# Projections of an attention and feed-forward kernel: x's tiles moved by 64 bytes, and 512 columns in one matmul instead of 256 in two

## The chip, the cores and the metric

The kernel runs on one core of a Trainium2 chip. The metric is the device time of one execution in microseconds (us), lower is better. Three runs of the kernel before took 1352.29, 1352.97 and 1356.74 us; the median is 1352.97 us.

## The reference, cut to what matters

```python
# attention inside chunks of 64 positions, 8 batches, 8 heads, 576 positions, head size 64
scores = scale * np.matmul(q_c, k_c.transpose(0, 1, 2, 4, 3))
attn = softmax(scores)                          # over the 64 keys of the chunk
x = np.matmul(attn, v_c) as (4608 tokens, 512)  # heads joined
# first feed-forward block: three projections of x, their maximum, one projection back
h = np.maximum(np.maximum(x @ w1, x @ w2), x @ w3)   # w1, w2, w3: 512 x 768
x = h @ w_out                                        # 768 x 512
# second block
h = np.maximum(x @ w_in, 0.0)                        # 512 x 2048
out = h * h @ w_out                                  # 2048 x 512
```

The change touches only the line with `x @ w1`, `x @ w2` and `x @ w3`.

## The kernel before, in words

The 4608 tokens are cut into 9 blocks of 512 (`NB`, `TB`). Each block's x is held transposed: the 512 model dimensions lie on the partitions in four pieces (`KD` = 4) and the 512 tokens lie along the free axis. To keep nearly full float32 precision, every operand of a matmul is split in two float32r parts, a rounded one ("h") and the rest ("l"), and a product is the sum of three: h by h, h by l, l by h.

The work has four stages, in this order on TensorE (PE): attention and the three projections of the first block (line 445, tile p), the way back (line 647, tile y), and the second block's two products (lines 543 and 594, tiles z and o). The last three are done by a seven-product scheme on halves, so their matmuls have 256 columns by nature.

A **projection** is one call of `proj` (line 450): for one block b, one of six groups f of 128 output features and one of the three weights w, it fills one PSUM tile of 128 x 512 out of four pieces k and three pairs of parts. Each pair is a **pass** here: one weight tile of 128 x 128 against the block's 512 tokens. `halves` (line 439) issues a pass as two matmuls of 256 columns (`HC` = 256), each with its own load of the same weights (LDWEIGHTS, engine row PEld). There are 9 x 6 x 3 = 162 projections of 12 passes; the first two, p000 and p001, are computed in two parts of 256 tokens (`parts=2`, line 775) so that they can start when half of the block is there.

x's two tiles per block, `xh` and `xl`, are made in `att_V` (lines 404 to 407) in the pool `ap`, two buffers each. `att_H` (line 426, ScalarE) and `att_L` (line 431, VectorE) fill them from PSUM, 128 tokens at a time. Other tiles share the buffers later on: `hr` (line 608), `h3` and `h4` (line 622), and the wide operands of lines 278 to 283. The weights lie in the pool `wp`, in tiles of 2048 bytes per partition.

Addresses within a partition matter below. In the program as built every tile of `wp` begins at a multiple of 128 bytes. The three small pairs of tiles at line 64 take 192 bytes, so every later tile of `ap`, x's among them, begins 64 bytes past a multiple of 128. All slices that the matmuls read begin a multiple of 128 bytes further in, with one exception: where `early` is 48, slices begin 48 words earlier (lines 281 to 283 and 623), which is at a multiple of 128 again. Those are few matmuls of lines 543, 594 and 647.

What sets the order: up to block 1 a list written by hand (`order`, line 784) under a manual schedule. From block 2 on the loop at line 856 issues one projection per slot, one step of attention in four of 18 slots, and as many steps as the table `PACE` says of the generators that split the later weights (`park`, `park_wo`); there the framework's scheduler orders each engine's instructions and queues. After each projection `p1_end` (line 470) takes the PSUM tile: ScalarE copies the first weight's result (line 474), VectorE takes the maximum with the second and third (lines 477, 481), and the result goes to DRAM by SyncE's queue (lines 487, 490, 502).

Of the kernel before, what the change touches and what calls it, by code (L numbers as in the profile page):

```python
# [11 lines left out]
F32R = mybir.dt.float32r  # L12
# [8 lines left out]
P = 128  # L21
D = 64
H = 8
TB = 512
HC = 256
# [4 lines left out]
KD = 4  # L30
# [2 lines left out]
NM = 14  # L33
NG = 4
EARLY = 48
NJ = NF1 // 2
BY_HEADS = (0, 1, 4,)
FO = [f for j in range(NJ) for f in (j, NJ + j)]
QN = (1, 2, 5, 6, 3, 7, 4)
# [5 lines left out]
def kernel(ctx: ExitStack, tc, qkv, w123, w_out, w_in2, w_out2, out):  # L45


    nc = tc.nc
# [3 lines left out]
    ap = ctx.enter_context(tc.tile_pool(name="ap", bufs=2))  # L52
# [3 lines left out]
    def ps_tile(tag, name):  # L56
        return ps.tile([P, 512], F32, tag=tag, name=name, bufs={"acc": 4, "p": 2, "at": 2}[tag])
# [161 lines left out]
    def park_wo():  # L219
# [4 lines left out]
        for f in range(NF1):  # L224
            h, j = divmod(f, NJ)
            parts = [main[2 * r + h][:, j, :] if j < 2 else rest[r][:, h, :] for r in range(2)]
# [47 lines left out]
    def operands(wide, name, early=0):  # L274

        if not wide:
            return {}
        ts = [[ap.tile([P, KD, TB], F32R, tag=t, name=f"{name}{t}{i}") for i in range(2)] for t in ("xh", "xl")]
        ops = {i: [halved(ts[j][i // 4][:, i % 4, :]) for j in range(2)] for i in range(1, 8)}
        if early:  # L280
            ops[1] = [
                halved(t[0].rearrange("p k n -> p (k n)")[:, TB - early:2 * TB - early]) for t in ts
            ]
        return ops
# [14 lines left out]
    x_t = {}  # L299
# [100 lines left out]
    def att_V(*ts, tag="at"):  # L400
        for t in ts:
            b = t // 4
            if b not in x_t:
                x_t[b] = (
                    ap.tile([P, KD, TB], F32R, tag="xh", name=f"xh{b}"),
                    ap.tile([P, KD, TB], F32R, tag="xl", name=f"xl{b}"),
                )
            xps_t[t] = ps_tile(tag, "X").rearrange("p (a q) -> p a q", a=4)
        ops = [(t, et_t.pop(t), v_t.pop(t)) for t in ts]
        for p in range(4):  # L410
            for c in range(2):
                for t, et, v in ops:
                    for j in range(2):
                        o = (j ^ t % 2) * D
                        q = (c ^ t % 2) * D
                        nc.tensor.matmul(  # L416
                            xps_t[t][j * D:j * D + D, p, c * D:c * D + D], lhsT=v[o:o + D, c, p, :],
                            rhs=et[o:o + D, p, q:q + D], start=True, stop=True,
                        )
        for t in ts:  # L420
            if t >= 8:
                att_H(t)

    def att_H(t):
        o = t % 4
        nc.scalar.copy(x_t[t // 4][0][:, :, o * P:o * P + P], xps_t[t])
# [7 lines left out]
    def mm_k(dst, wpair, xpair, k, first, last):  # L434

        (wh, wl), (xh, xl) = wpair, xpair
        halves(dst, ((wh, xh), (wh, xl), (wl, xh)), first, last)

    def halves(dst, pairs, first, last):


        for j, (lhs, rhs) in enumerate(pairs):
            for i in range(dst.shape[-1] // HC):
                c = slice(i * HC, i * HC + HC)
                nc.tensor.matmul(  # L445
                    dst[:, c], lhsT=lhs, rhs=rhs[:, c], start=first and i == 0 and j == 0,
                    stop=last and j == len(pairs) - 1, skip_group_check=True,
                )

    def proj(wpair, xpair, name, parts=1, tag="p"):  # L450

        p = ps_tile(tag, name)
        wh, wl = wpair
        xh, xl = xpair
        n = TB // parts
        for i in range(parts):
            t = slice(i * n, i * n + n)
            for k in range(KD):
                a, c = k // 2, slice(k % 2 * P, k % 2 * P + P)
                mm_k(p[:, t], (wh[:, a, c], wl[:, a, c]), (xh[:, k, t], xl[:, k, t]), k, k == 0, k == KD - 1)  # L460
            if i + 1 < parts:
                yield None
        yield p


    h_t, st = {}, {}
    h_d = [dp.tile([7, P, NJ, HC], F32, name=f"hd{b}") for b in range(NB)]
    y_d = [dp.tile([P, KD, TB], F32, name=f"yd{b}") for b in range(NB)]
# [56 lines left out]
    def split_y(b, parts):  # L525

        ops = y_t[b] = operands(b % 2 == 1, "y", EARLY if b == 1 else 0)
        q = [parts[k][:, :, n * HC:n * HC + HC] for k in range(2) for n in range(2)]
# [40 lines left out]
    def load_g(b, g):  # L569
        parts = []  # L570
        for row in range(2):
            t = ap.tile([P, 2, 512], F32, tag="in", name="gr", bufs=4)
            nc.sync.dma_start(t, g_d[b][g, row])
            parts.append(t)
        return parts

    def split_g(parts, wide, early):

        ops = operands(wide, "g", early)
        q = [halved(parts[k][:, m, :]) for m in range(2) for k in range(2)]  # L580
        yield ops
        for i, x in combine(q, True, nc.vector):
            split_into(ops, i, x, "g")
            yield
# [16 lines left out]
    def load_h(b, part):  # L601
# [5 lines left out]
        for k in pairs:  # L607
            t = ap.tile([P, KD, TB], F32R, tag="xh", name="hr").bitcast(F32).rearrange("p k n -> p (k n)")
            t = t[:, 0:6 * HC].rearrange("p (i j n) -> p i j n", i=2, j=NJ)
            nc.sync.dma_start(t, h_d[b][k:k + 2].rearrange("i p j n -> p i j n"))  # L610
            raw_h[b, k], raw_h[b, k + 1] = t[:, 0], t[:, 1]
        for k in one:
            t = ap.tile([P, 2, 512], F32, tag="in", name="hr", bufs=4).rearrange("p k n -> p (k n)")
            t = t[:, 0:3 * HC].rearrange("p (j n) -> p j n", j=NJ)
            nc.sync.dma_start(t, h_d[b][k])
            raw_h[b, k] = t

    def split_h(b):

        for k, i in enumerate(QN):  # L620
            if i in (3, 4):
                t = ap.tile([P, KD, TB], F32R, tag="xl", name=f"h{i}").rearrange("p k n -> p (k n)")
                o = TB - (EARLY if b % 3 == 0 and i == 3 else 0)
                ts = [t[:, o + m * TB:o + m * TB + TB] for m in range(3)]
# [12 lines left out]
    def yq(b, i, tag, first):  # L637
# [5 lines left out]
        for a in range(2):  # L643
            c = slice(a * P, a * P + P)
            for j in range(NJ):
                for k, (l, r) in enumerate(((wh, hh), (wh, hl), (wl, hh))):
# [44 lines left out]
    def steps(t0, t1):  # L691
# [19 lines left out]
        def outputs(t):  # L711
            att_V(t, t + 1)
            att_L(t)
            att_L(t + 1)
            if t < 12:
                att_load(t + 4)
                att_load(t + 5)
            if t + 2 < t1:
                scores(t + 2)
# [20 lines left out]
    first = tc.manual_schedule()  # L740
# [4 lines left out]
    def tile_steps(k):  # L745

        att_load(k)
        yield
        att_S(k, tag="acc")
        yield  # L750
        m, n = (by_heads if k in BY_HEADS else att_M)(k), att_N(k)
        for _ in range(2):
            next(m)
        yield
        next(m, None)
        yield
        for _ in range(2 if k in BY_HEADS else 3):
            next(n)
        yield
        next(n, None)  # L760
        yield
        tp = att_T(k, "at")
        yield
        att_E(k, tp)
        yield
        att_V(k, tag="acc")
        yield
        att_H(k)
        yield
        att_L(k)  # L770
        yield
# [29 lines left out]
    for token in order:  # L801
# [6 lines left out]
        kind, n = token.rstrip("0123456789"), token.lstrip(ascii_letters)  # L808
# [10 lines left out]
        else:  # L819
            b, f, w = map(int, n)  # L820
# [35 lines left out]
    for b in range(2, NB):  # L856
        for slot in range(3 * NF1):
            f, w = divmod(slot, 3)
# [23 lines left out]
    last = None  # L882
# [43 lines left out]
    for b in range(NB):  # L926
        for g in range(NG):
# [27 lines left out]
            if b == NB - 1 and g == 0:  # L955
                parts = {j: load_g(*groups[j]) for j in range(2)}
                more = split_g(parts.pop(0), True, EARLY)
                ops = next(more)
# [67 lines left out]
```

## Time and profile before

| what | value |
|---|---|
| time of three runs | 1352.29, 1352.97, 1356.74 us |
| median | 1352.97 us |
| span of the profiled execution (the page gives no other time of it) | 1354.5 us |
| PE busy | 1337.8 us, 99% of the span |
| VectorE (DVE) busy | 979.8 us, 72% |
| ScalarE (ACT) busy | 556.9 us, 41% |
| GpSimd (POOL) busy | 178.4 us, 13% |
| bytes moved by DMA | 282.92 MB, mean 209 GB/s |

How to read it: the span runs from the first to the last instruction of the profiled execution. A matmul's row has a start and a duration, but matmuls are pipelined, so durations overlap and a busy share near 100% says nothing about how fast columns go in. The rate is read from the distance between the starts of two matmuls that follow each other. PEld is the row of the weight loads, which run beside the matmuls.

### The profile page before, as it was taken

The page shows a single profiled execution, that of the slowest core. Times are in us where ns is not written, and L with a number is a line of the kernel's source. Part 1 is how long each engine was busy: PE and PEld are TensorE (multiplying, and loading weights), DVE is VectorE, ACT ScalarE, POOL GpSimd, SP SyncE. Part 2 cuts the span into 40 slices and gives each one's busy share as a digit, 9 for nine tenths or more (in the row PEclk, how much of TensorE's full clock was granted, in tenths as well). Part 3 has the DMA queues.
Part 4 walks back from the last instruction along what each step waited for, and adds up shares of the span by engine and source line. Part 5 has one row for each costly group of instructions (what it writes and reads, how often), then busy time and mean ns, then how long its engine had stood idle before and what let it go on. Part 6 is the DMA issues. An engine that isn't in the chain of part 4 may idle for free.

```text
span 1354.5 us, 33080 instructions
## 1 busy us (share of the span) xinstructions
PE 1337.8 (99%) x13536; PEld 1325.1 (98%) x13537; DVE 979.8 (72%) x1661; ACT 556.9 (41%) x1047; POOL 178.4 (13%) x165
## 2 busy tenths in 40 slices
PE   7999999999999999999999999999999999999998
PEld 6999999999999999999999999999999999999998
DVE  6777789778898843566666666666777887887774
ACT  5632344344444422565433333333344453454442
POOL 2321035342344300000000000000001000000000
PEclk8999999999999999999999999999999999999999
DMA  9445779899788778998944333433597444443440
GB/s 271 124 140 158 227 228 313 256 319 292 256 284 270 253 253 301 381 308 270 294 167 143 122 139 135 149 140 141 211 355 284 148 147 137 144 156 125 141 141 32
DMA packets 146631, 282.92 MB, mean 209 GB/s; under 512 B 14384, under 2 KB 57008, under 8 KB 146480
## 3 DMA queue, kind: packets, MB, share of 16 engines
q1 hardware_dynamic: 146208, 280.55, 61.1%
q8 instruction: 106, 1.74, 0.5%
q14 instruction: 45, 0.37, 0.1%
q10 hardware_dynamic: 272, 0.26, 0.1%
HBM read 164.50 MB, written 116.26 MB: 207 GB/s over the span
## 4 chain that ended last, share of the span: by engine, by line
PE 91%; DVE 4%; DMA 3%; issue 1%; ACT 1%; SPq 0%; POOLq 0%; DVEq 0%; ACTq 0%
PE p L445 29%; PE z L543 25%; PE o L594 25%; PE y L647 8%; PE X L416 1%; DMA k<-in_qkv 1%; PE S L334 1%; PE T L388 1%; DMA hr<-hd 1%; DMA yr<-yd 0%; DMA wo20d<-pl 0%; DVE sm L373 0%; DVE e L361 0%; DVE e L382 0%; DVE a L107 0%
## 5 line engine op out<-in xcount | busy, mean ns | idle before, releaser
L543 PE MATMUL z<-yh,wih 128*128 128x256 f32 x560 | 154.7, 276 | 0.0
L543 PE MATMUL z<-yl,wih 128*128 128x256 f32 x560 | 154.6, 276 | 0.0
L543 PE MATMUL z<-yh,wil 128*128 128x256 f32 x560 | 154.6, 276 | 0.0
L594 PE MATMUL o<-wo2h,gxl 128*128 128x256 f32 x504 | 139.1, 276 | 0.0
L594 PE MATMUL o<-wo2h,gxh 128*128 128x256 f32 x504 | 139.1, 276 | 0.0
L594 PE MATMUL o<-wo2l,gxh 128*128 128x256 f32 x504 | 139.1, 276 | 0.0
L594 PE MATMUL o<-wo2h,gh 128*128 128x256 f32 x504 | 139.1, 276 | 0.0
L594 PE MATMUL o<-wo2l,gh 128*128 128x256 f32 x504 | 139.1, 276 | 0.0
L594 PE MATMUL o<-wo2h,gl 128*128 128x256 f32 x504 | 139.1, 276 | 0.0
L566 DVE TENSOR_TENSOR c<-z,s 128x512 f32<-128x512 f32 x108 | 74.3, 688 | 77.7 <-PE z L543 74.0
L566 POOL TENSOR_TENSOR u<-u,s 128x512 f32<-128x512 f32 x9 | 12.5, 1389 | 845.2 <-DVE u L566 674.7
L543 PE MATMUL z<-yxh,wih 128*128 128x256 f32 x448 | 123.8, 276 | 0.0
L543 PE MATMUL z<-yxh,wil 128*128 128x256 f32 x448 | 123.7, 276 | 0.0
L543 PE MATMUL z<-yxl,wih 128*128 128x256 f32 x448 | 123.7, 276 | 0.0
L551 ACT COPY s<-z 128x512 f32<-128x512 f32 x108 | 63.5, 588 | 139.0 <-PE z L543 124.2
L543 PEld LDWEIGHTS z<-yh,wih 128*128 128x128 f32 x560 | 105.1, 188 | 0.2 <-DVE c L566 0.2
L543 PEld LDWEIGHTS z<-yh,wil 128*128 128x128 f32 x560 | 105.1, 188 | 0.0
L543 PEld LDWEIGHTS z<-yl,wih 128*128 128x128 f32 x560 | 105.1, 188 | 0.0
L119 POOL TENSOR_TENSOR q<-a,r 128x256 uint32<-128x256 uint32 x76 | 66.6, 898 | 223.4 <-DVE a L107 100.1
L594 PEld LDWEIGHTS o<-wo2h,gxl 128*128 128x128 f32 x504 | 94.6, 188 | 0.0
L594 PEld LDWEIGHTS o<-wo2h,gxh 128*128 128x128 f32 x504 | 94.6, 188 | 0.0
L594 PEld LDWEIGHTS o<-wo2l,gxh 128*128 128x128 f32 x504 | 94.6, 188 | 0.0
(175 smaller groups left out, 4113.0 us busy)
## 6 DMA issues: line engine op xcount, KB each, us to landing
gd<-g SPq DMA_DIRECT2D x144, 256.0 KB, 2.0
gr<-gd SPq DMA_DIRECT2D x72, 512.0 KB, 3.6
qk<-in_qkv SPq DMA_DIRECT2D x28, 512.0 KB, 4.9
hr<-hd SPq DMA_DIRECT2D x17, 768.0 KB, 6.5
raw<-in_w_out SPq DMA_DIRECT2D x22, 512.0 KB, 4.6
hr<-hd SPq DMA_DIRECT2D x29, 384.0 KB, 5.8
raw<-in_w SPq DMA_DIRECT2D x18, 512.0 KB, 5.0
v<-in_qkv SPq DMA_DIRECT2D x72, 128.0 KB, 4.0
```

The source lines that it names most:

```text
L119: nc.gpsimd.tensor_tensor(out=part.bitcast(U32), in0=au[:, c], in1=ru[:, c], op=ALU.add)
L334: nc.tensor.matmul(s_t[t][o:o + D, h ^ t % 2, :], lhsT=q[r, h, :], rhs=k[r, h, :], start=True, stop=True,)
L388: nc.tensor.transpose(tp[:, p * P:(p + 1) * P], e[:, 2 * p:2 * p + 2, :].rearrange("p h k -> p (h k)"), ident)
L416: nc.tensor.matmul(xps_t[t][j * D:j * D + D, p, c * D:c * D + D], lhsT=v[o:o + D, c, p, :], rhs=et[o:o + D, p, q:q + D], start=True, stop= ...
L445: nc.tensor.matmul(dst[:, c], lhsT=lhs, rhs=rhs[:, c], start=first and i == 0 and j == 0, stop=last and j == len(pairs) - 1, skip_group_ch ...
L543: nc.tensor.matmul(dst[:, a * HC:a * HC + HC], lhsT=l[:, a, w], rhs=r[:, k, :], start=first and a + k + j == 0, stop=j == 2, skip_group_ch ...
L551: nc.scalar.copy(t, bank[tag])
L566: (eng or nc.vector).tensor_tensor(out=t, in0=x, in1=y, op=ALU.add)
L594: nc.tensor.matmul(bank[i][:, m * HC:m * HC + HC], lhsT=l[:, a, t], rhs=r[:, a, :], start=g + m + a + j == 0, stop=g == NG - 1 and j == 2, ...
L647: nc.tensor.matmul(dst[:, a * HC:a * HC + HC], lhsT=l[j][:, c], rhs=r[j], start=first and a + j + k == 0, stop=k == 2, skip_group_check=True,)
```

## The change

A new constant `SHIFT` = 16 (words of 4 bytes). `xh` and `xl` are allocated 32 words longer and used from word 16 on, so that x begins at a multiple of 128 bytes, as the weights do. `halves` is gone: `mm_k` issues each pass as one matmul of the width of its target, 512 columns, or 256 in the two projections of two parts. The order of the three pairs and of the pieces k stays.

```diff
@@ -33,6 +33,7 @@
 EARLY = 48
+SHIFT = 16
 NJ = NF1 // 2
@@ -401,9 +402,9 @@
             if b not in x_t:
-                x_t[b] = (
-                    ap.tile([P, KD, TB], F32R, tag="xh", name=f"xh{b}"),
-                    ap.tile([P, KD, TB], F32R, tag="xl", name=f"xl{b}"),
+                x_t[b] = tuple(
+                    ap.tile([P, KD * TB + 2 * SHIFT], F32R, tag=t, name=f"{t}{b}")[:, SHIFT:SHIFT + KD * TB]
+                    .rearrange("p (k n) -> p k n", k=KD) for t in ("xh", "xl")
                 )
@@ -434,18 +435,12 @@
         (wh, wl), (xh, xl) = wpair, xpair
-        halves(dst, ((wh, xh), (wh, xl), (wl, xh)), first, last)
-
-    def halves(dst, pairs, first, last):
-
-
+        pairs = (wh, xh), (wh, xl), (wl, xh)
         for j, (lhs, rhs) in enumerate(pairs):
-            for i in range(dst.shape[-1] // HC):
-                c = slice(i * HC, i * HC + HC)
-                nc.tensor.matmul(
-                    dst[:, c], lhsT=lhs, rhs=rhs[:, c], start=first and i == 0 and j == 0,
-                    stop=last and j == len(pairs) - 1, skip_group_check=True,
-                )
+            nc.tensor.matmul(
+                dst, lhsT=lhs, rhs=rhs, start=first and j == 0, stop=last and j == len(pairs) - 1,
+                skip_group_check=True,
+            )
```

Of the 162 projections 160 change: 160 x 12 = 1920 passes, which are 3840 matmuls and 3840 weight loads before and 1920 of each now. The 48 matmuls of 256 columns of p000 and p001 stay, with x at its new place. Lines up to 435 move down by one; line 445 becomes 440, and lines behind it move up by five.

On PE the instructions keep their places. This is the end of one projection and the beginning of the next in the list written by hand (w_0h and w_0l are the two parts of a weight tile, T the transposes and X the products of the attention); before:

```order
L445 MATMUL p_714<-xh_325,w_0h 128x256 x2
L445 MATMUL p_714<-xl_326,w_0h 128x256 x2
L445 MATMUL p_714<-xh_325,w_0l 128x256 x2
L388 MATMUL T<-ident,e 128x128 x4
L416 MATMUL X<-et,v 64x64 x32
L445 MATMUL p_799<-xh_325,w_1h 128x256 x2
L445 MATMUL p_799<-xl_326,w_1h 128x256 x2
L445 MATMUL p_799<-xh_325,w_1l 128x256 x2
```

and now:

```order
L440 MATMUL p_714<-xh_325,w_0h 128x512
L440 MATMUL p_714<-xl_326,w_0h 128x512
L440 MATMUL p_714<-xh_325,w_0l 128x512
L389 MATMUL T<-ident,e 128x128 x4
L417 MATMUL X<-et,v 64x64 x32
L440 MATMUL p_787<-xh_325,w_1h 128x512
L440 MATMUL p_787<-xl_326,w_1h 128x512
L440 MATMUL p_787<-xh_325,w_1l 128x512
```

Each pair of rows has become one of double width; nothing has moved.

On DVE the scheduler puts some rows of blocks 2 to 7 in another order. The first place is in block 2, where the maximum h of a projection, the scaling of two attention tiles (e by rs) and the conversion of later weights (a) are interleaved; before:

```order
L382 TENSOR_TENSOR e<-e,rs 128x512
L378 RECIPROCAL rs<-sm 128x8
L104 TENSOR_SCALAR a<-a 128x512
L382 TENSOR_TENSOR e<-e,rs 128x512
L481 TENSOR_TENSOR h<-p_2525,m_2507 128x512
L107 SCALAR_TENSOR_TENSOR a<-raw,a 128x512
```

and now:

```order
L383 TENSOR_TENSOR e<-e,rs 128x512
L379 RECIPROCAL rs<-sm 128x8
L476 TENSOR_TENSOR h<-p_2057,m_2039 128x512
L383 TENSOR_TENSOR e<-e,rs 128x512
L105 TENSOR_SCALAR a<-a 128x512
L103 TENSOR_SCALAR a<-a 128x512
```

The maximum h has moved ahead of the second scaling of e, and one conversion behind it; no row is added or lost.

## Rows read from the trace of the kernel before

**Rows 1.** The page: span, busy times, and granted clock in 40 slices.
```profile
span 1354.5 us, 33080 instructions
PE 1337.8 (99%) x13536; PEld 1325.1 (98%) x13537; DVE 979.8 (72%) x1661; ACT 556.9 (41%) x1047; POOL 178.4 (13%) x165
...
PEclk8999999999999999999999999999999999999999
...
PE p L445 29%; PE z L543 25%; PE o L594 25%; PE y L647 8%; PE X L416 1%; DMA k<-in_qkv 1%; PE S L334 1%; PE T L388 1%; DMA hr<-hd 1%; DMA yr<-yd 0%; DMA wo20d<-pl 0%; DVE sm L373 0%; DVE e L361 0%; DVE e L382 0%; DVE a L107 0%
```
**Rows 2.** Line 445 alone: count, duration ns min/median/max, first and last start in us.
```profile
L445 PE MATMUL p<-xh,w_0h x216: 276/276/384, 29.6 to 491.1; 128*128 128x256 f32 x108
```
**Rows 3.** Waits of PE, 29 to 510 us: us in total, times, longest.
```profile
PE T L388 <- DVE e L382: 1.6, 2, 1.1
PE p L445 <- issue: 1.0, 2, 0.6
PE p L445 <- DVE m L477: 0.5, 1, 0.5
```
**Rows 4.** Chain of work that ended last: start us, us, what, number of instructions.
```profile
153.21 8.18 PE p L445 x72
```
**Rows 5.** Timeline of PE in block 1: start us, us, engine, line, what.
```profile
59.88 0.40 PE L445 MATMUL p<-xh,w_1h 128*128 128x256 f32 x2
...
61.77 0.40 PE L445 MATMUL p<-xh,w_1l 128*128 128x256 f32 x2
```
**Rows 6.** Windows, line 445 alone: stretch, its us, PE busy (matmuls), PEld, clock, DMA.
```profile
38.00:120.00 82.00, 77.37 (x648) 76.57 (x648) 1.00 0.48 146
120.00:160.00 40.00, 32.61 (x278) 31.89 (x279) 1.00 0.54 174
163.00:187.00 24.00, 22.64 (x188) 22.26 (x188) 1.00 0.61 185
```
**Rows 7.** Timeline of PE in block 2, across a wait of PE.
```profile
163.69 0.39 PE L445 MATMUL p<-xl,w_1h 128*128 128x256 f32 x2
163.92 0.39 PE L445 MATMUL p<-xh,w_1l 128*128 128x256 f32 x2
164.70 0.50 PE L445 MATMUL p<-xh,w_1h 128*128 128x256 f32 x2 [0.39 <-issue]
165.04 0.40 PE L445 MATMUL p<-xl,w_1h 128*128 128x256 f32 x2
```
**Rows 8.** Timeline of PE, line 543, operands 64 bytes apart modulo 128.
```profile
799.78 0.28 PE L543 MATMUL z<-yxh,wil 128*128 128x256 f32 x1
...
800.12 0.28 PE L543 MATMUL z<-yxh,wil 128*128 128x256 f32 x1
...
802.95 0.28 PE L543 MATMUL z<-yxh,wih 128*128 128x256 f32 x1
```
**Rows 9.** Timelines of PE, lines 543 and 594, operands at one offset modulo 128.
```profile
700.63 0.28 PE L543 MATMUL z<-yxh,wih 128*128 128x256 f32 x1
...
702.05 0.29 PE L543 MATMUL z<-yxh,wih 128*128 128x256 f32 x1
...
1008.63 0.28 PE L594 MATMUL o<-wo2h,gxh 128*128 128x256 f32 x1
...
1010.08 0.28 PE L594 MATMUL o<-wo2h,gxh 128*128 128x256 f32 x1
```
**Rows 10.** Timeline of PE, second and fourth warm-up matmul at full clock.
```profile
7.62 0.38 PE L732 MATMUL warm<-zero 128*128 128x512 bf16 x1
...
8.05 0.38 PE L732 MATMUL warm<-zero 128*128 128x512 bf16 x1
```
**Rows 11.** Timeline of PEld, line 543: weight loads beside the matmuls of rows 8.
```profile
800.12 0.19 PEld L543 LDWEIGHTS z<-yxh,wih 128*128 128x128 f32 x1
```
**Rows 12.** Windows, all engines: PE, PEld, DVE, ACT, POOL busy, clock, DMA share, GB/s.
```profile
188.00:220.00 32.00, 31.30 (x420) 30.71 (x413) 28.94 (x48) 13.36 (x26) 15.45 (x14) 1.00 0.86 291
...
252.00:284.00 32.00, 31.41 (x385) 31.01 (x384) 29.38 (x58) 14.10 (x25) 14.38 (x15) 1.00 0.82 265
```
**Rows 13.** Groups of instructions: count, busy us, mean ns, idle before.
```profile
L481 DVE TENSOR_TENSOR h<-p,m 128x512 f32<-128x512 f32 x54 | 36.8, 684 | 17.2 <-PE p L445 16.5
L382 DVE TENSOR_TENSOR e<-e,rs 128x512 f32<-128x512 f32 x28 | 19.2, 685 | 0.2
```
**Rows 14.** Groups on PE from 38 to 120 us: count, busy us, mean ns.
```profile
L445 PE MATMUL p<-xl,w_2h 128*128 128x256 f32 x48 | 9.6, 281 | 0.0
```

## The prediction

> **What bounds the kernel now.** I read the page first. PE is busy 1337.8 of 1354.5 us, and in the chain that ended last line 445, the projections, has 29% [rows 1]. The granted clock is at its upper level, 2.4 GHz, in all slices but the first, so 256 columns need at least 256 / 2.4 = 106.7 ns and 512 need 213.3 ns. Line 445 runs from 29.6 to about 508 us; one of its 18 operand names has 216 matmuls [rows 2], together 18 x 216 = 3888. PE waits for others in that stage for only about 4 us, 1.6 of them for VectorE [rows 3]. So the stage is bound by how fast PE takes projections, and what a pass saves or costs comes out nearly whole at the end: the later stages start when this one is through, and they are PE's too.
>
> How long does a pass take? Starts are what counts. Over 72 matmuls of the chain it is 8.18 / 72 = 113.6 ns each [rows 4], so a pass of two takes 227.2 ns. But there is a second pace: between 59.88 and 61.77 us there are 16 matmuls, 1.89 / 16 = 118.1 ns each [rows 5], a pass 236.2 ns. It lasts: the stretches 38 to 120 and 163 to 187 us run so, the one between them does not [rows 6], and the trace shows one change of pace right behind a wait of 0.39 us: steps of 0.23 us for two matmuls before it (163.69 to 163.92) and 0.24 after [rows 7]. The clock is 1.00 on both sides. I take it that the order in time of a weight load's reads and the running matmul's reads settles into one of two patterns.
>
> Addresses matter too. Line 543 with weights and moving data 64 bytes apart modulo 128 takes (802.95 - 799.78) / 28 = 113.2 ns [rows 8]. The few matmuls whose slices begin 48 words early, so that both operands lie at one offset, take (702.05 - 700.63) / 12 = 118.3 ns on line 543 and (1010.08 - 1008.63) / 12 = 120.8 ns on line 594 [rows 9]. Being at one offset costs 5 to 8 ns for 256 columns. This is the arrangement that the change gives the projections.
>
> The Trainium skill ("TensorE: Matmul & The Clock Gate", Part 2, step 1) says that TensorE reads weights and moving data through two independent ports and that loading the next weights takes nothing from the running matmul. By that rule the offset would be without effect and the shift worth 0; rows 9 against rows 8 disagree, by 5 to 8 ns, so the sum below doesn't use it, and its result stands as a rival.
>
> **The change part by part.** Now: the slow stretches hold 648 + 188 = 836 matmuls of line 445 [rows 6]; 24 of them are second parts of p000 and p001 and stay at 256 columns, the other 812 are 406 passes. 406 x 236.2 + 1514 x 227.2 ns = 95.9 + 344.0 = 439.9 us for the 1920 passes.
>
> One instruction for 512 columns: no float32r matmul of 512 columns stands in the trace, so its pace is bounded. Below: the warm-up matmuls have 512 columns, though of bf16: two steps from 7.62 to 8.05 us, 215 ns each [rows 10]; it can't be under 213.3. Above: nothing overlaps better than now and the same-offset price falls on every 256 columns, 2 x 120.8 = 241.6 ns. I take 213.3 ns for the columns and once what a 256-column matmul shows beyond its columns, 113.2 - 106.7 = 6.5 ns: 219.8 ns. This is nearest to the warm-up row, the only one of 512 columns. It supposes that the shift removes what the offset costs at this length, or that the price is hidden: the weight load now starts with the matmul, both at 800.12 us [rows 8, 11], and uncovered it takes 384 - 276 = 108 ns (the longest and the median duration of rows 2: the first matmul behind another shape has to wait for its weights). Beside 106.7 ns of columns it has no room to slip; beside 213.3 ns it has 105 ns. And the slow pace should go, since it needs a load that is only just in time. 1920 x 219.8 = 422.0 us, a gain of 17.9 us.
>
> 1920 weight loads and 1920 matmuls less to issue: nothing on PE waits for its sequencer beyond 1.0 us in this stage [rows 3], so I cost that at 0; it is covered by the running columns.
>
> The 48 matmuls of p000 and p001 stay short and come to one offset: 48 x 5 ns = 0.2 us more.
>
> VectorE's new order: where h goes ahead of the second scaling of e, that e is late by one row of 0.68 us [rows 13], and PE's transposes wait for e; today they do so twice, 1.6 us in all [rows 3]. In return h gives its PSUM tile back earlier, by the 0.69 us of e. The cover is the projections between. I take 1 us, with 0 and 2 as ends. SyncE's and GpSimd's queues change places of neighbours only; their transfers are waited for by later steps, and I take 0. ScalarE and VectorE write x 64 bytes further, the same number of elements: 0.
>
> Sum: 1354.5 - 17.9 + 0.2 + 1.0 = 1337.8 us of span. The profiled execution lies 1.5 us over the median of the runs, 1352.97; taken off, **1336.3 us**. Its own range, with 215 ns and with 222 ns a pass: 1327 to 1341.
>
> **The rivals.**
>
> *The load is hidden whole.* With 105 ns to spare, a collision only delays the load, and the columns run at the pace of rows 10: 1920 x 215 = 412.8 us, a gain of 27.1, 1327.1 us. For it: a load of 108 ns beside columns of 106.7 ns explains the 113 ns without any loss in the columns. Against it: in the slow stretch the matmuls' own rows last 281 ns instead of 276 [rows 14, 2], so the columns were held up as well. The skill's two ports (above) would give the same time. 0.18.
>
> *The price is per instruction, and the shift brings the dearer one.* If the running columns are held up once per weight load, as rows 9 may be read, a pass costs 213.3 + (120.8 - 106.7) = 227.4 ns: 436.6 us, a gain of 3.3, 1350.9 us: the two halves of the change cancel. For it: nothing in rows 9 shows that the same offset is ever good. Against it: rows 9 are of matmuls that have no room for the load. 0.18.
>
> *Slower: the price is per column.* If operands at one offset hold the columns up all along, 512 columns cost 2 x 118.3 to 2 x 120.8 = 236.6 to 241.6 ns: 454.3 to 463.9 us, 14.4 to 24.0 us more, so 1354.5 + 14.4 + 1.2 - 1.5 = 1368.6 to 1378.2 us. The place is every pass of line 440; it decides from 228.5 ns a pass on, (439.9 - 1.2) / 1920, where gain turns to loss. For it: rows 9 are the only ones with the operands so placed, and all are slower than their neighbours; float32r columns need twice the bytes of the bf16 columns of rows 10, so that row may promise too much. Against it: a weight load lasts 108 ns, and the second half of a long matmul has none beside it. 0.22.
>
> *VectorE becomes the bound.* It is busy 28.94 and 29.38 of 32 us in two stretches [rows 12], 0.90 and 0.92; a stage shorter by 17.9 / 440 = 4% brings that to 0.96. If each of the 12 pairs of attention tiles from block 3 on made PE wait 0.8 us, the mean of the two waits in rows 3, 9.6 us would go back: 1345.9 us. 0.05.
>
> **How the numbers follow.** The forecast has 0.37. The time predicted is that of the forecast, 1336 us. About 0.3%, 4 us, is what a measurement of this kernel can tell from no change. Faster by more: forecast, hidden load and VectorE, 0.37 + 0.18 + 0.05 = 0.60; within: 0.18; slower: 0.22. The range reaches down to the hidden load, 1327, and up into the slower rival, to 1372, which leaves out its dearer half, 0.11, and a few hundredths below.
>
> **What would show it.** Steps between starts on line 440: near 220 ns the forecast is right, 215 the hidden load, 227 the cancelling, 236 or more the slower rival. In the windows of 38 to 120 us there should be no second pace; if matmuls of one projection differ from those of another by 4% at clock 1.00, the patterns are still there. Lines 543, 594 and 647 should keep 113 ns. Waits of PE for VectorE above 3 us before the way back would speak for the last rival. The prediction is wrong if the passes take over 228.5 ns, or if PE's waits in this stage grow by more than 10 us.

## The result and the profile after

The changed kernel takes 1367.03 us (median of 6 runs, 1365.52 to 1369.32); the kernel before took 1354.62 us beside it (6 runs). The ratio is 1.0095, 95% interval 1.0079 to 1.0110: **the change makes the kernel slower by about 12 us**. The prediction was 1336.0 us, faster, with a range of 1327 to 1372.

The page of the changed kernel has these lines in the places of [rows 1]: span and busy times, granted clock, chain by line.

```profile
span 1363.5 us, 29241 instructions
PE 1349.3 (99%) x11616; PEld 1255.0 (92%) x11617; DVE 973.2 (71%) x1661; ACT 556.4 (41%) x1047; POOL 185.2 (14%) x165
...
PEclk9999999999999999999999999999999999999999
...
PE p L440 32%; PE z L538 26%; PE o L589 25%; PE y L642 8%; PE X L417 1%; PE S L335 1%; DMA k<-in_qkv 1%; PE T L389 1%; DMA yr<-yd 1%; SPq L308 0%; DVE e L362 0%; DVE mx L359 0%; DVE sm L374 0%; DVE e L383 0%; DVE xl L432 0%
```

The clock is at its upper level in all slices and PE is busy 99% as before, so the added time is time in which PE works more slowly. Which stage? The chain of the changed kernel (start us, us, what, number of instructions) has one long piece for each of the last two stages:

```profile
664.09 350.66 PE z L538 x2988
...
1017.61 337.58 PE o L589 x2977
```

and the chain of the kernel before has the same pieces:

```profile
666.80 338.96 PE z L543 x2988
...
1008.68 337.49 PE o L594 x2977
```

Here the loss stands: stage z, whose instructions the change doesn't touch, goes from 338.96 to 350.66 us, **11.7 us more**; stage o stays. Ahead of stage z the changed kernel is 2.7 us earlier (664.09 against 666.80), of which the projections have 1.1: they run from 27.8 to 529.5 us (501.7) where they ran from 29.6 to 532.4 us (502.8; the prediction's "about 508" for their end was misread). -2.7 + 11.7 = 9.0 us is the difference of the two spans, 1363.5 and 1354.5. The medians differ by 12.4 because the two profiled executions lie on different sides of them. A run's time is some 2 us more than its span: the profiled execution of the changed kernel took 1365.52 us, 1.5 under its median of 1367.03, and that of before about 1356, some 2 above 1354.62.

Stage z is slower matmul by matmul. The groups of instructions (count, busy us, mean ns) of the changed kernel:

```profile
L538 PE MATMUL z<-yh,wih 128*128 128x256 f32 x560 | 156.9, 280 | 0.0
...
L589 PE MATMUL o<-wo2h,gxh 128*128 128x256 f32 x504 | 139.2, 276 | 0.0
```

In the timeline of PE one sees where it begins:

```profile
696.34 0.28 PE L538 MATMUL z<-yl,wih 128*128 128x256 f32 x1
...
697.70 0.28 PE L538 MATMUL z<-yl,wih 128*128 128x256 f32 x1
...
697.93 0.28 PE L538 MATMUL z<-yxh,wih 128*128 128x256 f32 x1
...
701.47 0.28 PE L538 MATMUL z<-yh,wih 128*128 128x256 f32 x1
```

Up to 697.70 us there are 12 steps of 1.36 / 12 = 113.3 ns, from 697.93 on 30 steps of 3.54 / 30 = 118.0 ns. The first 12 of these are the first early slices, the 12 behind them the first that lie in a moved buffer. The stage stays at this pace. The windows of 740 to 780 us (stretch, its us, PE busy and matmuls, clock, DMA share, GB/s) of the changed kernel and of the kernel before:

```profile
740.00:780.00 40.00, 40.00 (x342) 1.00 0.34 124
```

```profile
740.00:780.00 40.00, 40.00 (x355) 1.00 0.37 136
```

342 matmuls instead of 355 in 40 us, at the same clock 1.00 and with less DMA traffic, not more. The waits of PE from 27 to 510 us (us in total, times, longest) answer to [rows 3] and have not grown:

```profile
PE T L389 <- DVE e L383: 1.8, 3, 1.1
PE p L440 <- DVE xl L432: 0.4, 1, 0.4
```

The passes of the projections, at last, run at two paces that change with the block. From the chain, 36 passes in blocks 2, 3 and 4:

```profile
150.36 8.17 PE p L440 x36
...
205.69 8.37 PE p L440 x36
...
262.07 8.17 PE p L440 x36
```

8.17 / 36 = 226.9 ns and 8.37 / 36 = 232.5 ns; over all of them the mean is 229.6 ns.

### The profile page after: what moved, and what is told of

It is laid out like the page before. It is cut to its first block, busy times and chain, and to the rows that moved or that the text cites. A ratio compares the mean times of both kernels' runs of the same rounds, so it can differ in the third digit from the quotient of the medians.

```text
span 1363.5 us, 29241 instructions
## 1 busy us (share of the span) xinstructions
PE 1349.3 (99%) x11616; PEld 1255.0 (92%) x11617; DVE 973.2 (71%) x1661; ACT 556.4 (41%) x1047; POOL 185.2 (14%) x165
## 4 chain that ended last, share of the span: by engine, by line
PE 94%; DMA 2%; DVE 2%; ACT 1%; issue 0%; SPq 0%; POOLq 0%; DVEq 0%; ACTq 0%
PE p L440 32%; PE z L538 26%; PE o L589 25%; PE y L642 8%; PE X L417 1%; PE S L335 1%; DMA k<-in_qkv 1%; PE T L389 1%; DMA yr<-yd 1%; SPq L308 0%; DVE e L362 0%; DVE mx L359 0%; DVE sm L374 0%; DVE e L383 0%; DVE xl L432 0%
## 5 line engine op out<-in xcount | busy, mean ns | idle before, releaser
L120 POOL TENSOR_TENSOR q<-a,r 128x256 uint32<-128x256 uint32 x76 | 73.6, 991 | 216.0 <-DVE a L108 104.4
L589 PEld LDWEIGHTS o<-wo2h,gh 128*128 128x128 f32 x504 | 94.6, 188 | 0.0
```

The source lines that it names most:

```text
L120: nc.gpsimd.tensor_tensor(out=part.bitcast(U32), in0=au[:, c], in1=ru[:, c], op=ALU.add)
L589: nc.tensor.matmul(bank[i][:, m * HC:m * HC + HC], lhsT=l[:, a, t], rhs=r[:, a, :], start=g + m + a + j == 0, stop=g == NG - 1 and j == 2, ...
```

## What differs between the blocks, and between the two stages z

Two buffers of x take turns block by block. The change makes each of the two tiles 32 words longer, so a tile's buffers lie 8320 bytes apart instead of 8192, and 8320 is 128 past a multiple of 256. Call the **distance** of a step the place where the running matmul's moving operand begins, less the place where the weights begin that are loaded beside it for the next matmul, modulo 256 bytes, from the addresses in the program as built. It counts modulo 256, not modulo 128 as was said ahead of the result. In the projections and in stages y and z the weights begin 128 bytes past a multiple of 256 in every kernel built here, so that there the distance changes with the moving operand's own place alone:

| steps | kernel before | changed kernel |
|---|---|---|
| projections (line 445, 440) | 192: all | 0: 1055 passes; 128: 864 passes |
| stage z (line 543, 538), wide operands in x's buffers | 192: 2975 | 192: 2447; 64: 528 |
| stage z, early slices | 0: 48 | 128: 48 |

The theory at this point: the distance sets the pace, the blocks at 128 are the dear ones, and stage z was slowed by the longer buffers, since they also hold its wide operands. The rivals: the 512-column instructions, or the new offset of x as such, do it.

## The experiments

The diffs are cut to the lines that matter.

**One part of the change alone (two kernels).** The first takes only the longer tiles, used from word 0, with passes in halves:

```diff
-                    ap.tile([P, KD, TB], F32R, tag="xh", name=f"xh{b}"),
-                    ap.tile([P, KD, TB], F32R, tag="xl", name=f"xl{b}"),
+                    ap.tile([P, KD * TB + 2 * SHIFT], F32R, tag=t, name=f"{t}{b}")[:, 0:0 + KD * TB]
```

> The kernel before with xh and xl only allocated 32 words longer: x stays 64 bytes past a multiple of 128 and every pass stays two matmuls of 256 columns, but the second buffer of xh and of xl begins 128 bytes, and the tiles behind them 512 bytes, later. Theory layout (stage z runs at the slow pace because its wide operands lie in these buffers at another place modulo 256): z at 117 to 118 ns a matmul, 11.6 us more, ratio about 1.008. Theory inherited pattern (z is slow because of what the long matmuls or the new offset leave behind on PE): z at 113.4 ns, ratio 1.000. Projections 113.3 or 117.8 ns in both.

Measured: 1377.34 us, ratio 1.0167 (1.0147 to 1.0186). Its chain in blocks 3, 4 and 6 and in stage z:

```profile
210.01 8.48 PE p L446 x72
...
267.09 8.48 PE p L446 x72
...
406.43 8.18 PE p L446 x72
...
675.46 351.07 PE z L544 x2976
```

64 unused words in two tiles cost more than the whole change, and about twice what was expected. Stage z takes 351 us as in the changed kernel, so neither the wide instructions nor the shift is needed for that. And the projections lose too: 8.48 / 72 = 117.8 ns a half in block 3, whose x lies at distance 64, but also in block 4 at 192, where the theory had 113.3; block 6, at 192 too, does run at 8.18 / 72 = 113.6 there.

The second takes only the 512-column passes, with x where it was:

```diff
-        halves(dst, ((wh, xh), (wh, xl), (wl, xh)), first, last)
+            nc.tensor.matmul(
+                dst, lhsT=lhs, rhs=rhs, start=first and j == 0, stop=last and j == len(pairs) - 1,
```

> The kernel before with each pass as one matmul of 512 columns, x where it was, 64 bytes from the weights' offset. It tells what the width does by itself. If columns of float32r are read at a fixed rate (113.3 ns per 256 whether a weight load runs or not), a pass takes about 227 ns and the ratio is 0.998 to 1.000. If the cost above the columns is per instruction, a pass takes 220 ns: 13 to 17 us less, ratio 0.988 to 0.990. If the offset of the change matters, passes are slower here than its 229.6 ns mean, 233 or more: ratio 1.005. Theory layout expects stage z at 113.4 ns here; theory inherited pattern expects 117 ns and 11.6 us more.

Measured: 1361.66 us, ratio 1.0051 (1.0030 to 1.0071). From its timeline, 36 passes apart:

```profile
47.21 0.40 PE L439 MATMUL p<-xh,w_1h 128*128 128x512 f32 x1
...
55.61 0.40 PE L439 MATMUL p<-xh,w_0h 128*128 128x512 f32 x1
```

8.40 / 36 = 233.3 ns a pass where two halves took 227.2 [rows 4], the third of the cases expected. Stage z stays at 338.96 us. So 512 columns at once are a loss at the old place, and a loss that spares stage z.

**The early slices (two kernels).** `EARLY` 32 instead of 48 puts the 48 early steps of stage z at distance 64, in the changed kernel and in the kernel before.

```diff
-EARLY = 48
+EARLY = 32
```

> The changed kernel with slices that begin 32 words early instead of 48, so that no matmul of stages y, z and o has both operands at one offset modulo 128. Theory kick (the 12 matmuls at one offset push stage z into the slow pace, and it does not come back): z at 113.4 ns, about 12 us less than the changed kernel, ratio to before about 1.000. Theory layout: z stays at 117 ns, ratio about 1.008.

> The kernel before with slices 32 words early instead of 48: 114 matmuls leave the arrangement of one offset. At 5 to 7 ns each that is 0.6 to 0.8 us less, ratio 0.9995, the same within noise; every theory expects stages z and o at 113.4 ns.

Measured: in the changed kernel 1359.94 us, ratio 1.0047 (1.0026 to 1.0067), some 7 us less and between the two expected; in the kernel before 1356.04 us, 1.0005 (0.9988 to 1.0022), no difference. The chain's piece of stage z in the first:

```profile
668.13 341.20 PE z L538 x2988
```

It is 2.2 us over the 338.96 of before, and the 576 steps at distance 64 (528 and the 48), at 117.8 instead of 113.4 ns, explain 2.5. The 2447 steps at 192 are back at the quick pace. So the other 9 us of the changed kernel's stage z are steps at distance 192 that are slow although their place is good: their mean there is 117.1 ns. **At distance 192 there are two paces, and something sets which.** The 48 early steps seem to take part in it.

Stage z gives back 9.5 us and the span only 5.5 (1363.5 to 1358.0). Of the other 4 us, 1.7 are a later start of the projections and 2.3 are lost in stage y. Its longest piece of the chain in this kernel and in the changed one:

```profile
531.60 118.31 PE y L642 x1005
```

```profile
529.91 80.42 PE y L642 x702
```

118.31 / 1005 = 117.7 ns a step against 80.42 / 702 = 114.6. Most steps of stage y lie at 192 in both. In the changed kernel its first 72 steps take 117.8 ns, and from behind its first 18 early ones, at distance 128, those at 192 take about 113.5. With `EARLY` 32 nothing lies at 0 or 128, and they stay at 117.8.

**The buffers a multiple of 256 bytes apart (two kernels).** Tiles 64 words longer instead of 32 (room for them comes from a tile of zeros, 512 bf16 elements shorter); in the second kernel also `EARLY` 64, which leaves no step of stages y and z at 0 or 128.

```diff
-    zero = const.tile([P, 1280], BF16, name="zero")[:, 0:512]
+    zero = const.tile([P, 768], BF16, name="zero")[:, 0:512]
-                    ap.tile([P, KD * TB + 2 * SHIFT], F32R, tag=t, name=f"{t}{b}")[:, SHIFT:SHIFT + KD * TB]
+                    ap.tile([P, KD * TB + 4 * SHIFT], F32R, tag=t, name=f"{t}{b}")[:, SHIFT:SHIFT + KD * TB]
```

> The change with slots 64 words longer in place of 32 (and the zero tile 512 words shorter, to make room), so that a second buffer lies a multiple of 256 bytes behind the first. Theory (distance of the moving operand from the weights, modulo 256 bytes, sets the pace): both buffers of x are at distance 0, all passes of the projections take 227.2 ns instead of 227.2 and 232.5 by turns; the wide operands of stages y and z are back where the kernel before had them, stage z is back at 113.4 ns a step. From after's 1367: 11.6 less for stage z and 835 passes x 5.3 ns = 4.4 less, about 1351, ratio to before 0.997. Rival (the 512-column instructions themselves, or the longer slots, slow stage z, wherever the buffers lie): stage z stays at 117.3 ns, about 1363, ratio 1.006.

Measured: **1350.41 us, ratio 0.9959 (0.9947 to 0.9971)**, with 1356.04 for the kernel before beside it: faster than both. From its chain, blocks 3 and 4 and stage z:

```profile
205.28 8.18 PE p L440 x36
...
260.73 8.17 PE p L440 x36
...
659.36 340.31 PE z L538 x2988
```

No more turns by block (227.2 and 226.9 ns a pass), and stage z is back, but for its first 323 steps, which in this execution took 117.8 ns each until the first early steps. The rival, by which wide passes or longer tiles slow stage z wherever they lie, falls: both are in this kernel.

> As the kernel with slots 64 words longer, and EARLY 64 instead of 48, so that the early slices of stage z also have their moving operand 64 bytes under the weights modulo 256 and no step at a distance of 0 or 128 is left in stages y and z. Theory (distance sets the pace): the 48 steps at some 118 to 120 ns become 113.4, and 4 runs of steps that stay slow behind them go: some 0.5 us less than with EARLY 48, about 1350.5, ratio 0.9965. Rival (the pace falls at these places for another reason, such as the buffer that changes there): the same four dips in stage z, no less time.

Measured: a median of 1358.78 us, ratio 1.0016 (0.9989 to 1.0044), and a miss: 12 runs fall into two groups, six from 1350.67 to 1355.08 and six from 1362.48 to 1365.85. The profiled execution is of the second group; its chain shows stages z and o:

```profile
662.38 338.64 PE z L538 x2988
...
1003.98 353.46 PE o L589 x3001
```

Stage z is as quick as expected, and stage o, 353.46 / 3001 = 117.8 ns a step, is slow from its first to its last matmul, where the same instructions, at the same addresses but for 12 early ones, took 337.49 / 2977 = 113.4 in the kernel with `EARLY` 48. One layout, two groups of times some 12 us apart, and 3022 steps x 4.4 ns are 13: the place decides only which paces there are.

**Pace by distance (two measuring kernels).** The kernel with tiles 64 words longer, in which x begins at another word in each block; the second with its passes in two halves.

```diff
+START = (56, 16, 0, 8, 16, 24, 32, 40, 48)
-[:, SHIFT:SHIFT + KD * TB]
+[:, START[b]:START[b] + KD * TB]
```

> A measuring kernel: the change with slots 64 words longer, in which x begins at another word in each of its nine blocks, so that the distance of x from the weights modulo 256 bytes is 160, 0, 192, 224, 0, 32, 64, 96, 128 in blocks 0 to 8. Theory (distance modulo 256 sets the pace of a 512-column pass): 227.2 ns at 0, 233.3 at 192 and 232.5 at 128, as seen; 64 is expected at 235 or more (twice 117.8), 32, 96, 160 and 224 between their neighbours. Rival (it is the buffer of the pair, or the block's own place in the program, that goes slow, not the distance): two paces that go by turns with the block, whatever the distance.

> A measuring kernel: the same nine distances with the passes in two halves of 256 columns. Theory (distance modulo 256 sets the pace): a half takes 119.8 ns at 0, about 119 at 128, 117.8 at 64 and 113.3 at 192 (perhaps 117 where slow steps stand ahead of it), and 32, 96, 160 and 224 lie between. Rival (buffer or place): two paces by turns, whatever the distance.

Measured, mean ns between starts (418 or more halves, 183 or more passes each):

| distance | 0 | 32 | 64 | 96 | 128 | 160 | 192 | 224 |
|---|---|---|---|---|---|---|---|---|
| a half of 256 columns | 119.9 | 116.8 | 117.8 | 119.9 | 118.7 | 117.6 | 113.6 | 118.3 |
| a pass of 512 columns | 227.2 | 233.4 | 229.1 | 233.5 | 233.4 | 234.1 | 233.3 | 233.2 |

In the chain of the kernel with halves, the blocks at distances 192, 224, 0, 32, 64 and 96 read so:

```profile
151.70 8.18 PE p L447 x72
...
209.59 8.52 PE p L447 x72
...
266.93 8.62 PE p L447 x72
...
326.76 8.41 PE p L447 x72
...
383.40 8.48 PE p L447 x72
...
440.53 8.63 PE p L447 x72
```

The rival of two paces by turns falls. The numbers at 0, 128 and 192 came as expected; 64 for a pass did not (229.1, expected 235 or more), and of 32, 96, 160 and 224 only some lie between their neighbours. Each of the two kernels ran once, 1356.63 and 1367.69 us, and each distance but 0 had one block; those at 0, 64, 128 and 192 agree with other kernels here. **The best place of one length is a bad place of the other**: halves want 192, where passes of 512 columns cost 233.3, and passes want 0, where halves cost 119.9. At its best a pass is no quicker than two halves at theirs, 227.2 against 2 x 113.6.

**What makes the slow pace stay (three kernels).** If 12 steps in a row at distance 128 leave PE slow and 12 at 0 leave it quick, then `EARLY` 16, which exchanges 0 and 128, must cure the changed kernel and spoil the one with tiles 64 words longer. `EARLY` 64 in the kernel before takes all such steps out of its stages y and z.

```diff
-EARLY = 48
+EARLY = 16
```

> The change with EARLY 16 instead of 48: the 48 early steps of stage z lie at distance 0 instead of 128 modulo 256, and nothing else changes its distance. Theory (at distance 192 there are two paces, 113.3 and 117.8 ns; which of them holds persists until something disturbs TensorE, and 12 steps in a row at distance 128 leave it at the slow one, at distance 0 at the quick one): stage z slows inside the early runs and at the 528 steps at distance 64 alone and comes back to 113.3 behind them, z about 114.3 ns a step in the mean, 9 us less than the change, about 1358, ratio 1.003. Rival (the 528 steps at distance 64 that the change brings keep stage z slow): z stays at 117.3, 1367.

> The kernel with slots 64 words longer, its early steps at distance 128 instead of 0; no step of stage z lies at distance 64. Theory (12 steps in a row at distance 128 leave TensorE at the slow pace): stage z at 117.8 ns from its first early run to its end, some 2700 steps x 4.4 ns = 12 us more than with EARLY 48, about 1362, ratio 1.005. Rival (it takes the steps at distance 64 to keep it slow): no dearer than with EARLY 48, 1350.

> The kernel before with EARLY 64, so that all steps of stages y and z are at distance 192 and all of the last stage's main line at 64, none at 0 or 128. Theory (two paces at one distance, and whichever a wait of TensorE leaves it at stays until the next wait): nothing in stage z brings it back, the executions fall into two groups, some 1352 and some 12 to 13 us more (3024 steps x 4.4 ns), as they did with slots 64 words longer and EARLY 64. Rival (the two groups come from the wide passes or the longer slots): one group at the kernel before's time less 0.5, about 1353.

Measured: the changed kernel is not cured, 1366.58 us, ratio 1.0083 (1.0056 to 1.0109), stage z 351.96 us. It is slow from its 50th step on, long before the first early one. The one with longer tiles takes 1365.64 us, 1.0074 (1.0051 to 1.0098), near the 1362 expected, but for another reason. From its chain:

```profile
662.28 339.01 PE z L538 x2988
...
1004.22 350.64 PE o L589 x2977
```

Its stage z is quick; stage o begins with 10 steps of 113.5 ns, then come its 12 early ones at distance 128, and it is slow from there to its end. So the theory of this pair falls for stage z in both kernels and fits stage o of the second. In the changed kernel, whose stage o has the same 12 steps, the slow pace ends 24 steps behind them, with the next 12 at 192. The kernel before with `EARLY` 64 took 1359.10 us, ratio 1.0050 (1.0010 to 1.0090), in two groups, as expected: five runs from 1351.45 to 1354.87 us and five from 1363.33 to 1369.70. Its profiled execution is of the quick group and shows one thing more, in the windows of the projections, line 445 alone (PE busy and matmuls, clock):

```profile
38.00:120.00 82.00, 76.00 (x661) 1.00 0.46 147
120.00:160.00 40.00, 32.36 (x276) 1.00 0.60 185
163.00:187.00 24.00, 21.42 (x187) 1.00 0.60 187
```

The first holds 661 matmuls in 76.00 us of PE where [rows 6] have 648 in 77.37: the slow stretch on which the prediction built is not there, though `EARLY` doesn't touch the projections. In the kernel before with `EARLY` 32 about a quarter of the steps of blocks 3 and 4 are slow, where the kernel before has next to none. So the slow stretch is one of its execution and not of the kernel. With 836 matmuls x 4.5 ns it is worth 3.8 us there; the other runs of before were not traced.

Put together, stage z over the kernels:

| steps at 64 beside those at 192 | early steps at | stage z, us | kernel |
|---|---|---|---|
| none | 0 | 338.96, 340.31 | before, wide passes alone and both measuring kernels; tiles 64 words longer |
| none | 128 | 339.01 | tiles 64 words longer, `EARLY` 16 |
| none | 192 | 338.91, 338.64 | `EARLY` 64: before; tiles 64 words longer |
| 48 | 64 | 338.88 | before, `EARLY` 32 |
| 528 | 64 | 341.20 | change, `EARLY` 32 |
| 528 | 128 | 350.66, 351.07, 352.00 | change; longer tiles alone; shift without wide passes (below) |
| 528 | 0 | 351.96 | change, `EARLY` 16 |

Each time is from one execution. The buffers decide the loss: with 528 steps at 64 and early ones at 0 or 128 the stage took 351 to 352 us in all four kernels, without steps at 64 never more than 340.31.

That it takes both, the steps at 64 and the early ones, is what the table suggests and the traces don't show. Only in the changed kernel do early steps turn a quick stage z slow. With longer tiles alone and with `EARLY` 16 it turns slow some 50 steps in, behind single steps of 186 to 257 ns, and with the shift alone it is slow from its first step, so there the early steps can't have started it. The change with `EARLY` 32 is quick from the first step, and may be quick for that reason: one of its ten runs took 1370.38 us and was not traced. And in stage y of the changed kernel early steps at 128 end the slow pace. In the traces, a stage z with 528 steps at 64 that was once slow never came back, and the one without them that began slow came back at its first early steps. What sets the pace, and why it holds, stays open.

**The shift without the wide passes.**

```diff
+                    ap.tile([P, KD * TB + 2 * SHIFT], F32R, tag=t, name=f"{t}{b}")[:, SHIFT:SHIFT + KD * TB]
```

> The kernel before with the change's longer slots and x's shift, its passes still in two halves: the change without its 512-column instructions. Theory (distance sets the pace, and an instruction of 512 columns saves only what a bad distance costs at each of its halves): halves at distance 0 cost 119.9 and at 128 118.7 ns, a pass 239.8 or 237.4 instead of 227.2 or 232.5, so 1055 x 12.6 + 864 x 4.9 = 17.5 us more than the change, about 1384. Rival (the halves carry no such cost, and the 512-column instruction is the slow one): 1350 to 1360.

Measured: 1387.10 us in one run, close to the 1384 expected; halves at distances 0 and 128 take 119.3 ns in the mean, stage z 352.00 us. The rival of a slow 512-column instruction falls: beside this place it is the cheaper form, by some 20 us.

## Why the prediction was wrong, point by point

The forecast was 16.7 us less, and 12.4 us more was measured. Two steps make up the 29 us between them: the term that the sum lacks, 11.7 us, and the term for the passes, 17.9 + 0.9 = 18.8 us.

- **"Lines 543, 594 and 647 should keep 113 ns"** failed for line 543, and it is what made the kernel slower. The sum has no term for the longer tiles, because it read the change as a move of x alone. Line 538 went to 117.3 ns a step, 11.7 us in all. Longer tiles moved the second buffers of every tile that shares them, and with them operands of a later stage. The kernel with the longer tiles alone shows this, the one with buffers a multiple of 256 apart shows it undone.
- **"1920 x 219.8 = 422.0 us"** was mis-sized: 229.6 ns in the mean, 440.8 us, so the forecast gain of 17.9 us was a loss of 0.9 against the 439.9 of before, and the prediction's own sign of being wrong, passes over 228.5 ns, came true. That the stage is 1.1 us shorter all the same has mostly to do with PE's waits, 2.2 us in all instead of 3.7. That a matmul's overhead of 6.5 ns is paid once for 512 columns is what failed: 227.2 - 213.3 = 13.9 ns at distance 0 and 19.2 at 128 (232.5 ns in the changed kernel). Nor is the cost simply one per column or one per load: at 0 a half pays 119.9 - 106.7 = 13.2 and a pass 13.9, as if per load, but at 192 a half 6.9 and a pass 20.0.
- **The offset, read modulo 128**, was too coarse. Distances 64 and 192 are one class modulo 128, and halves take 117.8 and 113.6 ns there. [rows 8] were steps at 192 and [rows 9] steps at 0; no row of the kernel before on line 445 or 543 was at 64 or 128.
- **"The slow pace should go"** held where the distance is 0: with both buffers there, 227 ns in all blocks. That two orders of reads make the two paces, as the prediction supposed, no run shows. And the 95.9 us of slow passes in the sum were one execution's; 3.8 us of the expected gain need not be there in another run of before.
- **48 halves at one offset, 0.2 us**: 119.8 ns each instead of 113.4, 0.3 us. Right.
- **VectorE's order, 1 us**: PE waited 1.8 and 0.4 us for VectorE instead of 1.6 and 0.5 [rows 3], so 0.1 us. It lies within the ends given, and the rival of VectorE as the bound falls with it.
- **The hidden load (215 ns)** falls: the best of eight distances gave 227 ns. The Trainium skill ("TensorE: Matmul & The Clock Gate", Part 2, step 1) has weights and moving data on two independent ports, by which the distance would be without effect. The trace disagrees: 113.6 to 119.9 ns for the same half at eight places.
- **The price per instruction (227.4 ns)** had the right number for the passes at distance 0, 227.2, and didn't foresee that half of the blocks lie elsewhere.
- **The slower rival** gave 1368.6 to 1378.2 us and came near the time by another way. Its price of 236.6 ns or more was never reached; 229.6 is just past its turning point of 228.5, and the loss is in stage z. The range held the time by luck: the slower rival, which stretched it that far, looked for the loss in the passes.

## What to carry to other kernels

An allocation that grows by a few words moves every buffer behind it and every other tenant of the same slots: list the addresses of all matmul operands before and after, and look at stages that the change doesn't name. Where weights are loaded beside a running matmul, take the place of both operands modulo 256 as a parameter, measure the pace for each length of matmul, and don't expect the best place of 256 columns to serve 512. When one group of instructions shows two durations at one clock in one trace, a second execution has to show whether that is the kernel or the run.

## What the runs showed of the hardware that was not expected

- A float32r matmul of 512 columns with a weight load of its own took 227 ns a step at best here, 213.3 being its columns at 2.4 GHz; the bf16 warm-up matmuls, each with a load too, took 215 [rows 10].
- Its pace has a period of 256 bytes in the distance of moving operand and weights: two blocks at distance 0 that differ by 256 modulo 512 took 227.3 and 227.1 ns a pass. Of the eight places tried one is good for each length: 192 for 256 columns (113.6 ns, others 116.8 to 119.9), 0 for 512 (227.2, others 229.1 to 234.1). As the weights stayed at one place modulo 256, the moving operand's own place would explain these numbers as well as the distance.
- The distance doesn't tell all: on lines 589 and 594, where weights and moving data have exchanged their pools, steps at 64 can take 113.4 ns; halves of the projections and steps of stage z there took some 118 in every trace.
- At a place with a quick pace there is a slow one as well (113.4 and 117.8 ns), and one of them can hold for 3000 steps. Two kernels without any early step at 0 or 128 in stages y and z fell into two groups of times, half of the runs in each, whose medians lie some 12 and 16 us apart; one execution of each kernel was traced. What chooses, a wait of PE or what the steps ahead of it leave behind, is not settled.
